# A fused attention, expert and dense kernel: joined weight blocks, a reordered attention loop, dense weights kept in SBUF, and a deferred low part

## The chip, the cores and the metric

The kernel runs on one core of a Trainium2 chip. The metric is the device time of one execution in microseconds (us). The engines are TensorE (PE in the profile, PEld its weight loads), VectorE (DVE), ScalarE (ACT), GpSimd (POOL) and SyncE (SP, which here only issues DMAs).

## The reference

Three layers follow one another, over 3072 tokens of 384 numbers.

```
state = alpha[t] * state + outer(k[t], v[t]);  y[t] = q[t] @ state      # 4 x 8 heads, 768 steps, 48 wide
e = argmax(cosine(x, expert_emb) / tau)                                 # 8 experts, one per token
x2[token] = gate[token] * (relu(x[token] @ w1[e]) @ w2[e])              # w1: 384 x 1024, w2: 1024 x 384
h = x2 @ w_in;  g = where(h > 0, h, exp(min(h, 0)) - 1);  out = g @ w_out   # 384 x 2048, 2048 x 384
```

w_in and w_out come as 64-bit floating point numbers, all else as 32-bit ones.

## The kernel before

**Attention stage.** The sequence is cut into 24 tiles of 128 steps. For a tile, two scans on VectorE make running products of alpha (R backwards, line 316, and A forwards, line 325), GpSimd scales k and q by them (Kh, line 321, and Qh, line 328), TensorE makes scores (psS, line 352), VectorE masks them from PSUM into P (line 354, two halves), and TensorE makes the output (psY), the state's update (psU) and the router's logits (psX). ScalarE copies. Every step writes its instructions by hand in one order (`manual_schedule`), and each engine takes its own in that order. In the loop of `fast()` one turn i issues: transpose of tile i+1 (`stT`), both scans of tile i+2 (`stA`) with the state's addition, router steps and the scatter of one finished tile (`put`) between them, then the scores and masks of tile i+1 (`stB`), and the outputs of tile i (`stC`). Router arithmetic comes as a list of small VectorE instructions, of which `step(n)` issues n. `put` copies the token number on GpSimd (line 522) and scatters 128 rows to a DRAM buffer sorted by expert (line 523).

**Expert stage.** `moe1` takes 64 blocks (8 experts by 8 parts of 128 hidden units). Numbers are kept as a rounded high part and a low part, so each product is three matmuls: block n issues nine of 432 columns into `h` (`mm1`), then nine of block n-1 into `y` (`mm2`). ScalarE writes the high part `hh` (line 886) and VectorE the low part `hl` (line 887), which the next `mm2` needs. Expert weights come in slots of 128 x 1536 (768 KB), two staging buffers deep, and are split in three pieces a slot: high on ScalarE (line 175), low on VectorE (line 178), into rings of eight slots; w1 and w2 have slots of their own.

In the same blocks the dense layer's 64-bit weights are turned into 32-bit ones, in 32 parts (`decode`: three integer instructions on VectorE, lines 212 to 214, a square on ScalarE, line 216, two on GpSimd) and split (`decode_end`: line 226 on ScalarE, line 227 on VectorE). Both parts are then stored to DRAM (lines 229 and 230), and in the last two experts loaded back into the ring by GpSimd's queue (`load_dense`). The buffers that a part is decoded in (`dt`, `dg`) number two; a third decode needs the first one's stores to have read them.

**Dense stage.** `moe2` takes 96 blocks (six groups of 512 tokens by 16 parts). Block n is nine matmuls of 512 columns into one of four PSUM buffers, a minimum on VectorE (`mn`, line 1032), an exponential on ScalarE, a combination on VectorE (`g`, line 1035), and high and low parts (`gh`, line 1038, `gl`, line 1039); then the twelve matmuls of block n-3 into `o`.

Of the kernel before, what the change touches and what calls it, by code (L numbers as in the profile page):

```python
# [20 lines left out]
T = 128  # L21
# [18 lines left out]
SLOT = 1536  # L40
XW = DM + 1
# [14 lines left out]
def fused_kernel(ctx, tc, qk, a, v, emb, w1, w2, wi, wo, cst, sel, cols, out):  # L56
# [5 lines left out]
    ring = ctx.enter_context(tc.tile_pool(name="ring", bufs=8))  # L62
    stage = ctx.enter_context(tc.tile_pool(name="stage", bufs=2))
# [76 lines left out]
    wq = []  # L140
    for e in range(E):
        for s in range(2):
            wq.append(("w1", e, s, w1[e, :, s * SLOT:(s + 1) * SLOT]))
        for s in range(2):
            wq.append(("w2", e, s, w2[e, :, s * SLOT:(s + 1) * SLOT]))
    raw, whi, wlo = {}, {}, {}
    nload = [0]

    def load_w(n=1):
        for _ in range(n):  # L150
            if nload[0] < len(wq):
                nm, e, s, src = wq[nload[0]]
                t = stage.tile([128, SLOT], F32, tag="raw", name="raw")
                nc.sync.dma_start(out=t, in_=src)
                raw[nload[0]] = t
                nload[0] += 1

    PIECES = 3
    pieces = [(i, j) for i in range(len(wq)) for j in range(PIECES)]
    npc = [0]  # L160

    def split_piece(lag=None):

        if npc[0] >= len(pieces):
            return
        i, j = pieces[npc[0]]
        npc[0] += 1
        nm, e, s, _ = wq[i]
        if j == 0:
            whi[nm, e, s] = ring.tile([128, SLOT], F32R, tag="whi", name="whi")  # L170
            wlo[nm, e, s] = ring.tile([128, SLOT], F32R, tag="wlo", name="wlo")
        w = SLOT // PIECES
        sl = slice(j * w, (j + 1) * w)
        h, l, r = whi[nm, e, s], wlo[nm, e, s], raw[i]
        nc.scalar.activation(out=h[:, sl], in_=r[:, sl], func=AF.Copy)  # L175
# [12 lines left out]


    HS = SLOT // 4  # L190
    dq = [(nm, j, src) for nm, src in (("wi", wi), ("wo", wo)) for j in range(4 * SLOT // HS)]
    d_hi = {nm: dram.tile([128, 4 * SLOT], F32, name=nm + "_hi") for nm in ("wi", "wo")}
    d_lo = {nm: dram.tile([128, 4 * SLOT], F32, name=nm + "_lo") for nm in ("wi", "wo")}
    dbuf = {}
# [8 lines left out]
    dpart = {}  # L203

    def decode(j, pool):
        if j >= len(dq):
            return
        w = dbuf.pop(j).bitcast(I32).rearrange("p (n two) -> p n two", two=2)
        lo, hi = w[:, :, 0], w[:, :, 1]
        t = pool.tile([128, HS], I32, name="dt")  # L210
# [8 lines left out]
        dpart[j] = (g, tf)  # L219

    def decode_end(j):
        if j not in dpart:
            return
        nm, s, _ = dq[j]
        g, tf = dpart.pop(j)
# [6 lines left out]
    def load_dense(nm, s):  # L232
        whi[nm, 0, s] = ring.tile([128, SLOT], F32R, tag="whi", name="whi")
        wlo[nm, 0, s] = ring.tile([128, SLOT], F32R, tag="wlo", name="wlo")
        nc.gpsimd.dma_start(out=whi[nm, 0, s], in_=d_hi[nm][:, s * SLOT:(s + 1) * SLOT])
        nc.gpsimd.dma_start(out=wlo[nm, 0, s], in_=d_lo[nm][:, s * SLOT:(s + 1) * SLOT])

    def wblk(nm, e, col, n):
        s, c0 = divmod(col, SLOT)
        return whi[nm, e, s][:, c0:c0 + n], wlo[nm, e, s][:, c0:c0 + n]  # L240
# [19 lines left out]
    def attention():  # L260
        with ExitStack() as st:
# [4 lines left out]
            xp = st.enter_context(tc.tile_pool(name="xp", bufs=8))  # L266
# [12 lines left out]
            ones = gp.tile([128, 1], F32, name="ones")  # L279

# [21 lines left out]
            Qh, Kh, Rs = {}, {}, {}  # L302

            def stA(i, mid):

# [4 lines left out]
                if i >= NT:  # L310
                    mid()
                    return
                al = at.pop(i)
                R = Rs[i] = wk.tile([C2, SW], F32, name="R")
                A = wk.tile([C2, SW], F32, name="A")
                nc.vector.tensor_tensor_scan(R[:, ::-1], al[:, ::-1], back[:, ::-1], 0.0, op0=ALU.mult, op1=ALU.max)
                fo = fore[i % 2]
                nc.vector.reciprocal(seg(fo)[:, :, 0:1], seg(R)[:, :, 1:2])
                x = qkt.pop(i)
                Kh[i] = wk.tile([C2, NP, T], F32, name="Kh")  # L320
                nc.gpsimd.tensor_tensor(Kh[i], x[:, 1], R[:, 1:].rearrange("c (p t) -> c p t", t=TP)[:, :, 1:], op=ALU.mult)
                step(2)
                if i < NT - 2:
                    mid()
# [5 lines left out]
                if i >= NT - 2:  # L330
                    mid()
# [838 lines left out]
```

## Time and profile before

| | us |
|---|---|
| median of 3 runs (889.39 to 891.69) | 891.16 |
| the profiled execution | 883.97 |
| its span, first to last instruction | 882.2 |
| attention stage, to 202.5 | 202.5 |
| expert stage, 202.5 to 473.4 | 270.9 |
| dense stage, 473.4 to 882.2 | 408.8 |

Busy over the span: TensorE 819.9 us (93%), VectorE 565.3 (64%), ScalarE 356.5 (40%), GpSimd 207.8 (24%). A TensorE that is busy need not be at its peak, since the end of a matmul is modelled and the granted clock changes. A `[4.27 <-ACT hh L886]` behind a row says that the engine stood idle for 4.27 us before it and that ScalarE's instruction of line 886 released it.

### The profile page before, as it was taken

What the parts mean: (1) busy time and instruction counts of PE and PEld (TensorE: products, weight loads), DVE (VectorE), ACT (ScalarE), POOL (GpSimd) and SP (SyncE); (2) the same over time, 40 slices, a digit from 0 to 9 for tenths busy, and PEclk for the clock granted to TensorE, in tenths of its full rate; (3) what the DMA queues carried; (4) which work ended last, traced back from release to release, by engine and by line L of the source; (5) the groups of instructions that cost most, each with busy time, mean ns of one, the idle gap of its engine ahead of it and who ended that gap; (6) DMA issues with size and microseconds to landing.
All of it is one profiled execution on the core that took longest, in us unless ns stands there. A gap on an engine that the chain in (4) does not pass through costs nothing.

```text
span 882.2 us, 13140 instructions
## 1 busy us (share of the span) xinstructions
PE 819.9 (93%) x4880; PEld 736.4 (83%) x4880; DVE 565.3 (64%) x1054; ACT 356.5 (40%) x739; POOL 207.8 (24%) x235
## 2 busy tenths in 40 slices
PE   7999888749997988989999999999999999999995
PEld 5888777629986987978988999999999999999995
DVE  7899999935785676867734555555555555555552
ACT  2556654614453454545523333333333333333331
POOL 6435555531233233323431001101100100100102
PEclk7898888978998999999999999999999999999999
DMA  9977795235888778978999000000000000000000
GB/s 265 311 191 192 205 261 158 55 102 184 198 241 189 183 223 208 243 208 209 307 299 214 1 1 10 27 1 9 27 1 9 29 1 4 33 0 1 37 1 36
DMA packets 47554, 107.50 MB, mean 122 GB/s; under 512 B 11880, under 2 KB 26472, under 8 KB 47472
## 3 DMA queue, kind: packets, MB, share of 16 engines
q1 hardware_dynamic: 42096, 84.46, 36.0%
q0 software_dynamic: 5376, 22.04, 7.9%
q8 instruction: 41, 0.67, 0.3%
q14 instruction: 41, 0.34, 0.1%
HBM read 81.68 MB, written 24.81 MB: 121 GB/s over the span
## 4 chain that ended last, share of the span: by engine, by line
PE 62%; DMA 8%; DVE 4%; issue 1%; ACT 1%; SPq 0%; POOLq 0%; POOL 0%; DVEq 0%; ACTq 0%
PE h L1030 22%; PE o L1052 8%; PE o L1050 8%; PE o L1051 8%; DMA wi_lo<-dt 5%; DMA wo_lo<-dt 3%; PE y L897 3%; PE y L896 3%; PE y L898 3%; PE h L881 2%; PE h L883 2%; PE h L882 2%; DVE wlo L178 1%; DVE hl L887 1%; PE t L864 1%
## 5 line engine op out<-in xcount | busy, mean ns | idle before, releaser
L1033 ACT ACTIVATE mn<-mn 128x512 f32<-128x512 f32 x96 | 60.7, 632 | 182.4 <-DVE mn L1032 182.4
L1052 PE MATMUL o<-whi,gl 128*128 128x384 f32 x384 | 129.3, 337 | 0.0
L1050 PE MATMUL o<-whi,gh 128*128 128x384 f32 x384 | 129.3, 337 | 0.0
L1051 PE MATMUL o<-wlo,gh 128*128 128x384 f32 x384 | 129.1, 336 | 0.0
L1030 PE MATMUL h<-xh,whi 128*128 128x512 f32 x288 | 112.5, 391 | 0.6 <-ACT x2T L910 0.6
L1030 PE MATMUL h<-xh,wlo 128*128 128x512 f32 x288 | 113.0, 393 | 0.0
L1039 DVE TENSOR_TENSOR gl<-g,gh 128x512 fp32r<-128x512 f32 x96 | 66.6, 694 | 72.4 <-ACT gh L1038 72.4
L1030 PE MATMUL h<-xl,whi 128*128 128x512 f32 x288 | 112.9, 393 | 0.0
L1035 DVE SCALAR_TENSOR_TENSOR g<-mn,h 128x512 f32<-128x512 f32 x96 | 66.1, 689 | 72.6 <-ACT mn L1033 72.6
L1061 POOL DMA_INDIRECT out_dram<-ob,ids x24 | 23.7, 986 | 363.3 <-DVE gl L1039 243.8
L1038 ACT ACTIVATE gh<-g 128x512 fp32r<-128x512 f32 x96 | 60.7, 632 | 77.8 <-DVE g L1035 77.0
L1032 DVE TENSOR_SCALAR mn<-h 128x512 f32<-128x512 f32 x96 | 66.2, 690 | 37.4 <-PE h L1030 37.1
L896 PE MATMUL y<-hh,whi 128*128 128x432 f32 x192 | 73.3, 382 | 9.8 <-ACT hh L886 7.8
L897 PE MATMUL y<-hl,whi 128*128 128x432 f32 x192 | 71.8, 374 | 7.9 <-DVE hl L887 7.9
L178 DVE TENSOR_TENSOR wlo<-raw,whi 128x512 fp32r<-128x512 f32 x96 | 75.6, 810 | 3.8 <-ACT whi L175 3.8
L217 POOL TENSOR_SCALAR dg<-dg 128x384 f32<-128x384 f32 x32 | 41.4, 1293 | 151.6 <-ACT dg L216 151.6
L1050 PEld LDWEIGHTS o<-whi,gh 128*128 128x128 f32 x384 | 72.1, 188 | 3.9
L1051 PEld LDWEIGHTS o<-wlo,gh 128*128 128x128 f32 x384 | 72.1, 188 | 3.8
L1052 PEld LDWEIGHTS o<-whi,gl 128*128 128x128 f32 x384 | 72.1, 188 | 0.0
L898 PE MATMUL y<-hh,wlo 128*128 128x432 f32 x192 | 70.7, 368 | 0.0
L881 PE MATMUL h<-xh,whi 128*128 128x432 f32 x192 | 70.4, 367 | 0.0
L883 PE MATMUL h<-xh,wlo 128*128 128x432 f32 x192 | 69.9, 364 | 0.0
(205 smaller groups left out, 1542.4 us busy)
## 6 DMA issues: line engine op xcount, KB each, us to landing
raw<-in_w_dram SPq DMA_DIRECT2D x32, 768.0 KB, 5.2
qk<-in_qk_dram SPq DMA_DIRECT2D x24, 448.0 KB, 8.1
vt<-in_v_dram SPq DMA_DIRECT2D x24, 352.0 KB, 6.8
raw<-in_wi_dram SPq DMA_DIRECT2D x16, 384.0 KB, 4.1
raw<-in_wo_dram SPq DMA_DIRECT2D x16, 384.0 KB, 4.6
at<-in_alpha_dram SPq DMA_DIRECT2D x24, 226.2 KB, 7.2
xr<-xs SPq DMA_DIRECT2D x7, 576.0 KB, 11.2
wi_hi<-dg SPq DMA_DIRECT2D x16, 192.0 KB, 5.8
```

Source lines behind the costliest of these rows:

```text
L178: nc.vector.tensor_tensor(l[:, sl], r[:, sl], h[:, sl].bitcast(F32), op=ALU.subtract)
L881: nc.tensor.matmul(ps, wh, xh[:, kk], start=(kk == 0), stop=False)
L883: nc.tensor.matmul(ps, wl, xh[:, kk], start=False, stop=(kk == KD - 1))
L896: nc.tensor.matmul(acc[e][d], wh, hh, start=(f == 0), stop=False)
L897: nc.tensor.matmul(acc[e][d], wh, hl, start=False, stop=False)
L898: nc.tensor.matmul(acc[e][d], wl, hh, start=False, stop=(f == FB - 1))
L1030: nc.tensor.matmul(ps, l, x, start=(n == 0), stop=(n == len(terms) - 1))
L1032: nc.vector.tensor_scalar(mn, ps, 0.0, None, op0=ALU.min)
L1039: nc.vector.tensor_tensor(gl, g, gh.bitcast(F32), op=ALU.subtract)
L1050: nc.tensor.matmul(o_, gh[:, sl], wh, start=(f == 0), stop=False)
L1051: nc.tensor.matmul(o_, gh[:, sl], wl, start=False, stop=False)
L1052: nc.tensor.matmul(o_, gl[:, sl], wh, start=False, stop=(f == M - 1))
```

## The change

- **Weights.** w1 and w2 are joined in one array, a hidden block's w1 columns beside its w2 rows, so that a slot of 1536 columns holds two whole blocks. Loads are of a piece (512 columns, 256 KB), six staging buffers in all, and each split piece issues the load of the sixth after it. The rings have four slots. In the expert stage splits begin at block 3.
- **Dense weights.** The decoded 32-bit parts stay in SBUF (`dense`, 18 buffers of 128 x 768). `decode_end`, its stores and `load_dense` are gone. `split_dense` makes high and low parts: a few in the last expert blocks, the others in the first group of the dense stage, two in most blocks. 64-bit loads are issued a block later than their buffer's decode.
- **Attention loop.** `stA` becomes `stR` (scan R, Kh) and `stA` (scan A, Qh), `stB` becomes `stS` (scores) and `stP` (one mask). A turn issues scores first; VectorE's order becomes R, state, first mask, A, second mask, then router steps and the weights' low part. The scatter stands between the first mask and A. The token number is copied by ScalarE, and GpSimd writes a 1 x 1 zero (`tick`) in its place.
- **Dense stage.** A block's low part `gl` is issued behind the next block's minimum and exponential (`flush`). The first token group's input lies in tiles of 128 x 512 rather than 128 x 3 x 512.
- The expert input `xr` has a buffer of its own from the start, used for all experts.

```diff
-    ring = ctx.enter_context(tc.tile_pool(name="ring", bufs=8))
-    stage = ctx.enter_context(tc.tile_pool(name="stage", bufs=2))
+    ring = ctx.enter_context(tc.tile_pool(name="ring", bufs=4))
+    stage = ctx.enter_context(tc.tile_pool(name="stage", bufs=2 * PIECES))
...
         def low_part():
-            nc.vector.tensor_tensor(l[:, sl], r[:, sl], h[:, sl].bitcast(F32), op=ALU.subtract)
-            if j == PIECES - 1:
-                raw.pop(i)
-                if i != AHEAD - 1:
-                    load_w()
+            nc.vector.tensor_tensor(l[:, sl], r, h[:, sl].bitcast(F32), op=ALU.subtract)
+            load_w()
...
-    def decode_end(j):
...
-        nc.scalar.activation(out=g.bitcast(F32R), in_=tf, func=AF.Copy)
-        nc.vector.tensor_tensor(tf, tf, g, op=ALU.subtract)
-        sl = slice(s * HS, (s + 1) * HS)
-        nc.sync.dma_start(out=d_hi[nm][:, sl], in_=g)
-        nc.sync.dma_start(out=d_lo[nm][:, sl], in_=tf)
...
+    def split_dense(nm, m, dense):
...
+        nc.scalar.activation(out=h, in_=r, func=AF.Copy)
+        nc.vector.tensor_tensor(l, r, h.bitcast(F32), op=ALU.subtract)
...
             def put(i, apart=True):
...
-                nc.gpsimd.tensor_copy(x[:, DM:], c["tok"][:, i:i + 1])
+                if apart and puts:
+                    nc.gpsimd.memset(tick, 0.0)
...
+                    stS(i + 1)
                     stT(i + 1)
...
-                    stA(i + 2, mid)
-                    if putq and i >= tail - 2:
+                    stR(i + 2)
+                    stG(i - 1)
+                    stP(i + 1, 0)
+                    if putq and place[putq[0]][0] in gated:
                         put(putq.pop(0))
-                    stB(i + 1)
+                    stA(i + 2)
+                    stP(i + 1, 1)
...
-                split_piece()
-                if n % 2:
+                if n > 2:
                     split_piece()
+                    if n % 2:
+                        split_piece()
+                if freed:
+                    load_d(freed.pop(), dc)
                 j = (n - 2) * 4 // 7
                 if j >= 0 and j != (n - 3) * 4 // 7:
-                    decode_end(j - 1)
-                    decode(j, dc)
-                    load_d(j + 2, dc)
+                    decode(j, dc, dense)
+                    freed.append(j + 2)
...
                 nc.scalar.activation(out=mn, in_=mn, func=AF.Exp)
+                flush()
                 g = e_p.tile([128, U], F32, name="g")
...
-                nc.vector.tensor_tensor(gl, g, gh.bitcast(F32), op=ALU.subtract)
+                low.append(lambda: nc.vector.tensor_tensor(gl, g, gh.bitcast(F32), op=ALU.subtract))
...
+                    if u == 0:
+                        split_dense("wi", m + 4, dense)
+                        split_dense("wo", m + 2, dense)
```

What this makes of the order on an engine, at three places. First VectorE in one turn of the attention loop, one with router steps, before:

```order
L316 SCALAR_TENSOR_TENSOR R<-at,back 112x517
L318 RECIPROCAL fore_127<-R 112x4
L502 TENSOR_TENSOR t<-psR,oh 128x32
L503 TENSOR_REDUCE pos<-t 128x4
L391 TENSOR_TENSOR G_123<-psU,G_123 112x4x112
L421 TENSOR_REDUCE lg<-psX 128x8
L325 SCALAR_TENSOR_TENSOR A<-at,fore_127 112x517
L504 TENSOR_SCALAR pos_i<-pos 128x4
L100 TENSOR_SCALAR rs_y<-ss 128x4
L354 TENSOR_TENSOR P<-psS,cs 128x512
L101 TENSOR_SCALAR rs_y<-rs_y 128x4
```

and in such a turn of the changed kernel (psU, psX, psR and psS lie in PSUM):

```order
L311 SCALAR_TENSOR_TENSOR R<-at,back 112x517
L312 RECIPROCAL fore_126<-R 112x4
L394 TENSOR_TENSOR G_122<-psU,G_122 112x4x112
L358 TENSOR_TENSOR P<-psS,cs 128x512
L321 SCALAR_TENSOR_TENSOR A<-at,fore_126 112x517
L358 TENSOR_TENSOR P<-psS,cs 128x512
L424 TENSOR_REDUCE lg<-psX 128x8
L505 TENSOR_TENSOR t<-psR,oh 128x32
L506 TENSOR_REDUCE pos<-t 128x4
L507 TENSOR_SCALAR pos_i<-pos 128x4
```

One mask now stands between the scans, and all router steps stand behind the second mask. On GpSimd, a turn is Kh, copy, scatter, Qh before and Kh, tick, scatter, Qh now.

Second, SyncE's queue in the second expert's blocks, before (wi_hi and wi_lo are the DRAM copies of the dense weights):

```order
L229 DMA wi_hi<-dg 128x384
L230 DMA wi_lo<-dt 128x384
L200 DMA raw_5439<-in_wi_dram 128x384
L154 DMA raw<-in_w_dram 128x1536
L229 DMA wi_hi<-dg 128x384
L230 DMA wi_lo<-dt 128x384
```

and now:

```order
L156 DMA raw<-in_w_dram 128x512 x3
L196 DMA raw_5488<-in_wi_dram 128x384
L156 DMA raw<-in_w_dram 128x512 x3
L196 DMA raw_5581<-in_wi_dram 128x384
L156 DMA raw<-in_w_dram 128x512
```

Only loads are left in it. Third, VectorE in the first blocks of the dense stage, before:

```order
L1032 TENSOR_SCALAR mn<-h_8143 128x512
L1035 SCALAR_TENSOR_TENSOR g<-mn,h_8143 128x512
L1039 TENSOR_TENSOR gl<-g,gh 128x512
L1032 TENSOR_SCALAR mn<-h_8174 128x512
L1035 SCALAR_TENSOR_TENSOR g<-mn,h_8174 128x512
```

and now (wd holds decoded weights, dwi and dwo their high parts, dlo their low parts):

```order
L231 TENSOR_TENSOR dlo<-wd,dwo 128x384
L1046 TENSOR_SCALAR mn<-h_8250 128x512
L1054 TENSOR_TENSOR gl<-g,gh 128x512
L1050 SCALAR_TENSOR_TENSOR g<-mn,h_8250 128x512
L231 TENSOR_TENSOR dlo<-wd,dwi 128x384
L231 TENSOR_TENSOR dlo<-wd,dwo 128x384
L1046 TENSOR_SCALAR mn<-h_8285 128x512
```

`gl` of the block before stands between `mn` and `g`, and two low parts of weights behind `g`.

## Rows read from the trace of the kernel before

**Rows 1.** Stages: stretch, length, busy us (instructions) by engine, granted clock, DMA.
```profile
0.00:202.50 202.50, 167.73 (x1629) 142.07 (x1629) 172.20 (x430) 95.65 (x267) 97.04 (x107) 0.86 0.68 193
202.50:473.40 270.90, 252.59 (x1237) 231.12 (x1236) 179.92 (x307) 125.84 (x252) 81.88 (x79) 0.97 0.84 222
473.40:882.20 408.80, 399.61 (x2016) 363.20 (x2016) 213.20 (x318) 134.96 (x221) 28.92 (x50) 1.00 0.06 20
```

**Rows 2.** Waits of TensorE in the expert stage: total us, times, longest.
```profile
PE y L897 <- DVE hl L887: 7.9, 8, 1.7
PE y L896 <- ACT hh L886: 7.8, 4, 4.3
```

**Rows 3.** Groups of VectorE, expert stage: busy, mean ns, idle before, releasers.
```profile
L227 DVE TENSOR_TENSOR dt<-dt,dg 128x384 f32<-128x384 f32 x32 | 18.2, 570 | 1.3 <-ACT dg L226 1.2
...
L212 DVE TENSOR_SCALAR dt<-raw 128x384 int32<-128x384 int32 x32 | 16.0, 501 | 37.3 <-DMA wi_lo<-dt 18.8 <-DMA wo_lo<-dt 18.5
```

**Rows 4.** The same of ScalarE.
```profile
L216 ACT ACTIVATE dg<-raw 128x384 f32<-128x384 f32 x32 | 17.6, 549 | 41.0 <-DMA wi_hi<-dg 21.1 <-DMA wo_hi<-dg 12.5 <-issue 5.0
L226 ACT ACTIVATE dg<-dt 128x384 fp32r<-128x384 f32 x32 | 16.6, 517 | 6.5 <-POOL dt L218 6.4
```

**Rows 5.** Timeline around one stall of TensorE: start, length, instruction, idle before.
```profile
273.31 0.32 SPq L230 DMA_DIRECT2D wi_lo<-dt  x1
...
276.99 0.54 ACT L216 ACTIVATE dg<-raw 128x384 f32<-128x384 f32 x1 [7.08 <-DMA wi_hi<-dg]
...
278.00 0.73 PE L896 MATMUL y<-hh,whi 128*128 128x432 f32 x1 [4.27 <-ACT hh L886]
```

**Rows 6.** Stretches of the expert stage: its start, behind that stall, an undisturbed one.
```profile
200.00:205.00 5.00, 5.00 (x17) 4.42 (x18) 1.21 (x2) 1.06 (x2) 0.00 (x0) 0.50 0.69 224
...
280.00:285.00 5.00, 5.00 (x16) 4.61 (x17) 4.44 (x8) 0.98 (x2) 1.83 (x3) 0.57 0.78 193
355.00:380.00 25.00, 25.00 (x130) 23.19 (x129) 20.56 (x36) 14.67 (x30) 8.05 (x7) 1.00 0.89 214
```

**Rows 7.** Timeline of VectorE in one turn of the attention loop.
```profile
138.42 1.23 DVE L316 TENSOR_TENSOR_SCAN R<-at,back 112x517 f32<-112x517 f32 x1
...
140.71 1.35 DVE L325 TENSOR_TENSOR_SCAN A<-at,fore 112x517 f32<-112x517 f32 x1
...
142.11 0.68 DVE L354 TENSOR_TENSOR P<-psS,cs 128x512 f32<-128x512 f32 x1
142.71 1.88 DVE L101 TENSOR_SCALAR rs_y<-rs_y 128x4 int32<-128x4 int32 x1
144.62 0.17 DVE L105 SCALAR_TENSOR_TENSOR rs_t<-rs_y,ss 128x4 f32<-128x4 f32 x1
...
145.99 1.24 DVE L316 TENSOR_TENSOR_SCAN R<-at,back 112x517 f32<-112x517 f32 x1
```

**Rows 8.** Timeline of GpSimd in the same turn.
```profile
140.92 1.12 POOL L522 COPY xt<-cs 128x1 f32<-128x1 f32 x1
142.32 1.02 POOL L523 DMA_INDIRECT xs<-xt,pos_i  x1 [0.28 <-DVE rs_y L100]
143.36 1.19 POOL L328 TENSOR_TENSOR Qh<-qk,A 112x512 f32<-112x512 f32 x1
```

**Rows 9.** The attention loop as one stretch, columns as in the first group.
```profile
15.00:165.00 150.00, 133.61 (x1422) 118.62 (x1423) 144.55 (x290) 80.63 (x230) 73.36 (x71) 0.88 0.75 210
```

**Rows 10.** Two scatters in a row at the end of attention, GpSimd.
```profile
179.62 0.99 POOL L523 DMA_INDIRECT xs<-xt,pos_i  x1 [0.28 <-POOL xt L522]
...
181.08 0.99 POOL L523 DMA_INDIRECT xs<-xt,pos_i  x1 [0.28 <-POOL xt L522]
```

**Rows 11.** Timeline of the dense stage's first block, and TensorE's first use of gl.
```profile
475.92 0.69 DVE L1032 TENSOR_SCALAR mn<-h 128x512 f32<-128x512 f32 x1 [0.71 <-PE h L1030]
...
477.31 0.69 DVE L1035 SCALAR_TENSOR_TENSOR g<-mn,h 128x512 f32<-128x512 f32 x1 [0.70 <-ACT mn L1033]
...
478.03 0.63 ACT L1038 ACTIVATE gh<-g 128x512 fp32r<-128x512 f32 x1 [0.75 <-DVE g L1035]
...
482.21 0.34 PE L1052 MATMUL o<-whi,gl 128*128 128x384 f32 x1
```

More of the change, by code (lines that the diff above doesn't have):

```diff
@@ L137, in inv_norm1 @@
         return y, steps
[L140 to L145, printed above, removed]
+    wq = [(e, s) for e in range(E) for s in range(FB * FW // SLOT)]
+    pieces = [(e, s, j) for e, s in wq for j in range(PIECES)]
     raw, whi, wlo = {}, {}, {}
     nload = [0]
+    npc = [0]
     def load_w(n=1):
         for _ in range(n):
[L151 to L154, printed above, removed]
+            if nload[0] < len(pieces):
+                e, s, j = pieces[nload[0]]
+                t = stage.tile([128, PW], F32, tag="raw", name="raw")
+                nc.sync.dma_start(out=t, in_=w12[e, :, s * SLOT + j * PW:s * SLOT + (j + 1) * PW])
                 raw[nload[0]] = t
                 nload[0] += 1
-    PIECES = 3
-    pieces = [(i, j) for i in range(len(wq)) for j in range(PIECES)]
-    npc = [0]
     def split_piece(lag=None):
@@ L187, in split_piece, with wblk @@
             lag.append(low_part)
-    HS = SLOT // 4
+    def wblk(e, col, n):
+        s, c0 = divmod(col, SLOT)
+        return whi[e, s][:, c0:c0 + n], wlo[e, s][:, c0:c0 + n]
+    HS = DM
     dq = [(nm, j, src) for nm, src in (("wi", wi), ("wo", wo)) for j in range(4 * SLOT // HS)]
-    d_hi = {nm: dram.tile([128, 4 * SLOT], F32, name=nm + "_hi") for nm in ("wi", "wo")}
-    d_lo = {nm: dram.tile([128, 4 * SLOT], F32, name=nm + "_lo") for nm in ("wi", "wo")}
-    dbuf = {}
+    dbuf, dec, dhi, dlo = {}, {}, {}, {}
     def load_d(j, pool):
@@ L201, in load_d, with decode @@
             dbuf[j] = t
-    dpart = {}
-    def decode(j, pool):
+    def decode(j, pool, dense):
         if j >= len(dq):
             return
+        nm, s, _ = dq[j]
+        d, r = divmod(s * HS, DS)
+        if r == 0:
+            dec[nm, d] = dense.tile([128, DS], I32, tag="wd", name="wd")
+        t = dec[nm, d][:, r:r + HS]
         w = dbuf.pop(j).bitcast(I32).rearrange("p (n two) -> p n two", two=2)
         lo, hi = w[:, :, 0], w[:, :, 1]
-        t = pool.tile([128, HS], I32, name="dt")
         g = pool.tile([128, HS], F32, name="dg")
@@ L279, in attention @@
             ones = gp.tile([128, 1], F32, name="ones")
+            tick = gp.tile([1, 1], F32, name="tick")
             qkt, at = {}, {}
@@ L352, in stB, with stP @@
                         nc.tensor.matmul(s[h2][:, p], kh[rows, p], qh[rows, p], start=True, stop=True)
-                for h2 in range(2):
-                    nc.vector.tensor_tensor(P[i][:, h2], s[h2], c["tri"][:, None, :].to_broadcast([128, NP, T]), op=ALU.mult)
-                    step(2)
+            def stP(i, h2):
+                if i >= NT:
+                    return
+                if h2 == 0:
+                    P[i] = wk.tile([128, 2, NP, T], F32, name="P")
+                nc.vector.tensor_tensor(P[i][:, h2], sc[i][h2], c["tri"][:, None, :].to_broadcast([128, NP, T]), op=ALU.mult)
             yT = {}
@@ L625, in fast @@
                 nc.gpsimd.memset(zero, 0.0)
-                stA(0, lambda: None)
-                stH(0)
-                stA(1, lambda: None)
-                stH(1)
+                for j in range(2):
+                    stR(j)
+                    stA(j)
+                    stE(j)
+                    stH(j)
                 rows, rtau = emb_t[:, :2 * NP * HP], emb_t[:, 2 * NP * HP:]
@@ L754, in ending @@
                     put(j)
-                xr = stage.tile([128, 4, DM], F32, tag="raw", name="xr0")
+                xr = xr_p.tile([128, 4, DM], F32, name="xr")
                 load_rows(xr, 0, [0, 128, 256, DM], puts[:-1])
@@ L904, in mm2 @@
                         for nm in ("xh2", "xl2"):
-                            first.append(stage.tile([128, KD, U], F32R, tag="raw", name=nm))
+                            first.append([stage.tile([128, U], F32R, tag="raw", name=nm) for _ in range(KD)])
                     nc.scalar.activation(out=x2T[:, 0, bass.ds(o1, CAP)], in_=y[0], func=AF.Copy)
@@ L1009, in moe2, with flush @@
             x2, gb, acc, stores = {0: first}, {}, {}, []
+            low = []
+            def flush():
+                while low:
+                    low.pop()()
             def load_u(u):
@@ L1014, in load_u @@
                 if u % 2:
-                    xh, xl = (x_p.tile([128, KD, U], F32R, tag=nm, name=nm) for nm in ("xh2", "xl2"))
+                    xh, xl = ([x_p.tile([128, U], F32R, tag=nm, name=nm) for _ in range(KD)] for nm in ("xh2", "xl2"))
                 else:
-                    xh, xl = (stage.tile([128, KD, U], F32R, tag="raw", name=nm) for nm in ("xh2", "xl2"))
+                    xh, xl = ([stage.tile([128, U], F32R, tag="raw", name=nm) for _ in range(KD)] for nm in ("xh2", "xl2"))
                 for kk in range(KD):
@@ L1094, in fused_kernel @@
         with tc.manual_schedule():
-            first = moe1(x2T, *x0)
+            dense = es.enter_context(tc.tile_pool(name="dense", bufs=18))
+            first = moe1(x2T, *x0, dense)
             shared.close()
-            moe2(x2T, first)
+            moe2(x2T, first, dense)
 _OUTS = [((N, DM), "float32")]
```

190 lines of the change are left out of this document (97 added, 93 removed).

## The prediction

> **What bounds the kernel now.** I read the stages first [rows 1]. The dense stage takes 408.8 us, and TensorE is busy for 399.6 of them at full clock (the rest is the end of the last group): 4.16 us for each of 96 blocks. Nothing outside TensorE can shorten it. The expert stage takes 270.9 us, TensorE is idle for 18.3 of them and its clock is 0.97. In the attention stage VectorE is the fullest engine.
>
> Next the waits of the expert stage. TensorE waits for `hl` and `hh`, the two parts of a block's hidden units [rows 2]. That is not the cause: VectorE and ScalarE were late because both stood in the decoding of the dense weights, waiting for a DMA. Line 212 has 37.3 us of idle time in front of it, nearly all ended by the stores of wi_lo and wo_lo [rows 3]; line 216 has 41.0, of which 33.6 end with the stores of wi_hi and wo_hi [rows 4]. One case shows the chain [rows 5]: SyncE issues the store of wi_lo at 273.31, ScalarE stands for 7.08 us until a buffer is free, its `hh` comes late, and TensorE starts at 278.00 after 4.27 us. Behind that stall its clock is 0.57 and 16 matmuls go through in 5 us, where an undisturbed stretch has 130 in 25 us, or 5.2 a microsecond [rows 6]. So a stall is paid twice, in idle time and in the slower time behind it.
>
> Last the attention loop: 150 us of which VectorE is busy for 144.55 and TensorE for 133.61 [rows 9]. VectorE's share is not all work. In one turn, a small router instruction takes 1.88 us where its neighbour of the same size takes 0.17 [rows 7]. It ends at 144.59, and GpSimd's Qh, which reads two SBUF operands, ends at 144.55 [rows 8]: it was held until Qh let go. The masks P, which read one operand from PSUM, are not held beside GpSimd.
>
> **Expert stage.** It holds 1237 matmuls [rows 1]. At the undisturbed rate these take 1237 / 5.2 = 237.9 us, so 33.0 us of the stage are idle or slow. The change takes away what causes this: no store reads the decode buffers, so a third decode waits only for VectorE, ScalarE and GpSimd themselves. 64 stores and 16 loads leave the queues, and the weights' loads no longer stand behind them. Work goes too: line 227 (18.2 us of VectorE) and line 226 (16.6 us of ScalarE) move to other places [rows 3, 4]. What is left is (179.9 - 18.2) / 238 = 68% of VectorE's time and (125.8 - 16.6) / 238 = 46% of ScalarE's, and in the undisturbed stretch, with more than that on both, TensorE stood in nothing. What stays: the slow start, where 17 matmuls take 5 us [rows 6], about half of it in the stage, 1.5 us; and blocks in which two pieces, a decode and a turned input fall together, which I put at 2.5. Gain 33.0 - 1.5 - 2.5 = 29 us. At most it is 31.5; at least 15, if half of the waits come back in another form.
>
> The cover that shrinks is the ring, eight slots to four. A slot is refilled from the block in which its last matmuls have been issued, and is needed 3.5 blocks later, 3.5 x 3.7 = 13 us. The refill is three pieces. Low and high part of 384 columns take 0.57 and 0.52 us [rows 3, 4], so a piece of 512 some 1.45 and three 4.4 us. That fits three times over, and the six loads in flight cover as much again.
>
> **Attention loop.** The turn in the rows took 145.99 - 138.42 = 7.57 us [rows 7]. Its loss begins on GpSimd: the copy of the token number stood from 140.92 to 142.04 [rows 8], until scan A ended at 142.06; then came the scatter, 1.02 us, and only then Qh, which held VectorE until 144.55. With the copy gone the scatter can run beside A, if the `tick` is not held as the copy was. No row shows a GpSimd write beside a scan, so the price lies between that of the copy, 1.12 us, and its unhindered 0.1 to 0.2; I take the low end, since the tick reads nothing and the held instructions in these rows all read SBUF. Qh then starts at A's end. One mask, 0.6 us, and reductions out of PSUM hide half of it, and what follows is held for 0.5 to 0.7 us where it was 1.7: a gain of 1.0 in the 13 turns that the code gives a scatter, 13 us. Against it: a second mask has moved in front of A, so in the nine other turns, where two masks hid Qh, half a microsecond of it is bare, 4.5 us; and TensorE, 89% busy, will not always have the scores ready for the first mask, 1.5 us. Sum: 7 us gained. The bounds are 16, where TensorE's own busy time is reached, and a loss of 4, if the tick is held.
>
> The Trainium skill (SBUF — State Buffer, "Who interferes with whom") says that a VectorE instruction with two SBUF inputs contends with a GpSimd one that reads SBUF and not with one that only writes it. By it the tick passes and the sum stays 7; by the opposite the loop loses 4. The held copy agrees with its first half; its second half no row shows.
>
> **End of attention.** Eight scatters in a row are 181.08 - 179.62 = 1.46 us apart, 0.99 of it the scatter, 0.47 copy and gap [rows 10]. A tick on another tile needs no gap in front of the scatter. At most 8 x 0.47 = 3.8 us go, at least none if ScalarE, which now writes the token numbers, becomes late. I take 2, and the rest of this end, the first expert's rows from DRAM and the branches, unchanged.
>
> **Dense stage.** Deferring `gl` cannot itself gain time, since TensorE does not wait there. It makes room for the weights' splits in the first group. Worked out from one block [rows 11]: from `mn` to `g` 1.39 us, in which `gl` of the block before (0.69, as `g`) fits; from `g` to `gh` 0.72, `gh` 0.63, then two high parts of 0.517 [rows 4], so the second is done 475.92 + 1.39 + 0.72 + 0.63 + 1.03 = 479.69; the last low part takes 0.57 [rows 3], and the next `mn` can start at 480.26. That is 4.34 us a block against TensorE's 4.16: 0.18 x 12 blocks = 2.2 us behind. The next group's six input splits fall into block 8, some 3 x 0.69 = 2.1 us on VectorE. The cover is what TensorE leaves before it needs the first `gl`: 482.21 - (480.26 + 0.69) = 1.3 us. So 2.2 + 2.1 - 1.3 = 3 us lost. From nothing, if ScalarE's parts overlap better, to 10, if the two low parts stand one behind the other (0.57 more in each block). In the other 80 blocks VectorE has 2.1 us of work and nothing waits.
>
> **Sum.** -29 - 7 - 2 + 3 = -35 us. On the profiled execution's 883.97 that is 849; the three timed runs lie 7.2 us above it, by 0.8%, so I take the difference off their median: 856 us.
>
> **Rivals.**
> *The tick is held by scan A as the copy was.* For it: the copy was. Against: it reads nothing. The loop then loses 4: -29 + 4 - 2 + 3 = -24, 867 us.
> *The expert stage's waits return.* VectorE's heaviest blocks are as long as TensorE's, and a late `hl` stops `mm2` at once. Against: the undisturbed stretch carried more. Half the gain: -15 - 7 - 2 + 3 = -21, 870 us.
> *All covers hold:* expert stage -31.5, loop -16, end -3.8, dense 0: -51, 840 us.
> *The dense stage's first group is slower:* +10 in place of 3: 863 us.
> *Slower than before: the ring of four.* If ScalarE's first piece of a slot waits for `mm2` with other work behind it on that in-order queue, `hh` is late, TensorE stalls and its clock falls as behind 278 us. There are 32 slots. The other terms give 6, so the stage would have to reach 270.9 + 6, which is 37.5 us over 239.4, or 1.2 us a slot; at 2 us a slot it is 239.4 + 64 - 270.9 - 6 = +26, 918 us. Against it stands the cover of 13 us over 4.4.
>
> **How the numbers follow.** Forecast 50%, tick held 15%, waits return 14%, all covers hold 13%, dense stage slower 4%, ring slower 4%. The likeliest is 856. Its own range, with a few microseconds either way in the loop and the dense stage, is 849 to 864. For 8 in 10 I add the two cases around 868 and leave out most of the case at 840 and the slow one: 842 to 872. A difference within 0.3%, 2.7 us, can't be told from none. Only the ring case is slower, 4%; 2% for a mixture that ends within 0.3%; faster 94%.
>
> **What would show it.** In the changed profile: no DMA among what ends VectorE's and ScalarE's waits at the decode; the expert stage near 242 us with clock 1.0 after its first 5 us; the scatter starting before A ends, and router instructions of under 0.9 us beside Qh; the loop near 143 us; in the dense stage's first group, `gl` behind the next `mn` and TensorE waiting for `gl` or `g` by a few tenths in some blocks from about the seventh on. The prediction is wrong if TensorE still stalls for more than a microsecond at a time among the experts, if ticks last as long as A, or if the loop's turns with scatter stay at 7.5 us.

## The result and the profile after

The changed kernel takes 861.18 us (median of 4 runs, 858.38 to 864.15) where the kernel before takes 891.42 on the same chip: a ratio of 0.9646, with a 95% interval of 0.9581 to 0.9711. The forecast was 856, in a range of 842 to 872. The profiled execution took 860.85 us, with a span of 858.9. Its difference to the profile of before is 23.3 us of span; the medians differ by 30, since the profiled execution of before lay 7.2 us under its median and this one on it. The steps of the prediction are held against the two profiles, where 35 us were forecast; in which stage the other 7 us of the medians lie, no profile shows.

The stages of the changed kernel, as in [rows 1] (the borders are again the first matmul of the experts and of the dense layer):

```profile
0.00:199.96 199.96, 160.35 (x1628) 138.95 (x1628) 161.96 (x430) 100.68 (x291) 97.17 (x106) 0.85 0.70 200
199.96:450.26 250.30, 243.48 (x1237) 225.50 (x1236) 167.73 (x279) 114.07 (x224) 73.62 (x65) 1.00 0.61 149
450.26:858.90 408.64, 399.30 (x2016) 361.54 (x2016) 219.14 (x346) 146.59 (x249) 29.33 (x47) 1.00 0.03 12
```

Nearly all of it comes from the expert stage: 270.9 us became 250.3. The attention stage gave 2.5, the dense stage 0.2. In the expert stage TensorE's idle time fell from 18.3 to 6.8 us and its mean clock rose from 0.97 to 1.00. A little of that is chance: only in this profile did the stage begin at full clock (26 matmuls in 5 us); in that of before and in all those below it began with 16 to 21 at 0.53 to 0.75. What TensorE still waits for there, against [rows 2]:

```profile
PE y L907 <- ACT hh L897: 3.3, 2, 1.7
PE y L908 <- DVE hl L898: 2.9, 4, 0.8
```

So fewer and shorter waits, and the same two operands. The reason behind them is a new one. VectorE's and then ScalarE's waits for a DMA at the decode, where [rows 3] and [rows 4] had the stores of the decoded weights:

```profile
DVE wd L210 <- DMA raw<-in_wi_dram: 10.5, 4, 4.0
DVE wd L210 <- DMA raw<-in_wo_dram: 6.9, 4, 4.1
```

```profile
ACT dg L214 <- DMA raw<-in_wi_dram: 15.9, 5, 4.8
ACT dg L214 <- DMA raw<-in_wo_dram: 10.5, 5, 4.9
```

No store is among them any more, but the 64-bit weights themselves arrive late. One case, in the way of [rows 5]: SyncE, then VectorE, ScalarE and TensorE in the same stretch.

```profile
254.93 1.11 SPq L246 DMA_DIRECT2D xr<-xs  x2
256.74 0.33 SPq L156 DMA_DIRECT2D raw<-in_w_dram  x1
257.12 0.42 SPq L196 DMA_DIRECT2D raw<-in_wi_dram  x1
```

```profile
269.75 0.36 DVE L210 TENSOR_SCALAR wd<-raw 128x384 int32<-128x384 int32 x1 [4.01 <-DMA raw<-in_wi_dram]
```

```profile
269.81 0.55 ACT L214 ACTIVATE dg<-raw 128x384 f32<-128x384 f32 x1 [4.79 <-DMA raw<-in_wi_dram]
270.26 0.51 ACT L897 ACTIVATE hh<-h 128x432 fp32r<-128x432 f32 x1
```

```profile
270.83 0.46 PE L907 MATMUL y<-hh,whi 128*128 128x432 f32 x1 [1.58 <-ACT hh L897]
```

The load is issued at 257.12, a block behind the decode that freed its buffer (VectorE's last read of it ended at 254.82) and close behind the next expert's rows (`xr`). It takes 12.6 us, where the median of the sixteen loads of w_in is 4.4, and the decode gets it at 269.75. The `hh` of the running block stands behind the decode's `dg` on ScalarE, in program order, and TensorE waits for it. It is the chain of [rows 5] with a load in the place of a store.

The attention loop. GpSimd in the turn that answers to [rows 8], and VectorE in the same turn, which answers to [rows 7]:

```profile
139.51 0.09 POOL L527 MEMSET tick<- 1x1 f32 x1
139.76 1.78 POOL L528 DMA_INDIRECT xs<-xt,pos_i  x1 [0.16 <-issue]
141.56 1.20 POOL L323 TENSOR_TENSOR Qh<-qk,A 112x512 f32<-112x512 f32 x1
```

```profile
139.50 1.22 DVE L321 TENSOR_TENSOR_SCAN A<-at,fore 112x517 f32<-112x517 f32 x1
140.64 0.67 DVE L358 TENSOR_TENSOR P<-psS,cs 128x512 f32<-128x512 f32 x1
141.75 1.04 DVE L507 TENSOR_SCALAR pos_i<-pos 128x4 int32<-128x4 f32 x1
```

The tick passes beside A in 0.09 us, as forecast, and the scatter starts before A ends. But then the scatter takes 1.78 us in place of 1.02: scan A ends at 140.72, and Qh starts 0.84 us behind it instead of with it. The router instruction beside Qh takes 1.04 us; it was 1.88 [rows 7] and was to be under 0.9. This turn takes 7.35 us (scan R at 137.03 and at 144.38) in place of 7.57.

At the loop's start VectorE stands for the alphas, which it hardly did before:

```profile
33.36 1.24 DVE L311 TENSOR_TENSOR_SCAN R<-at,back 112x517 f32<-112x517 f32 x1 [3.73 <-DMA at<-in_alpha_dram]
```

Where the loop gained and lost is told by the starts of scan R, one in each of its 22 turns. The tenth and the last, before and then now:

```profile
70.27 1.22 DVE L316 TENSOR_TENSOR_SCAN R<-at,back 112x517 f32<-112x517 f32 x1
...
158.99 1.23 DVE L316 TENSOR_TENSOR_SCAN R<-at,back 112x517 f32<-112x517 f32 x1
```

```profile
72.94 1.23 DVE L311 TENSOR_TENSOR_SCAN R<-at,back 112x517 f32<-112x517 f32 x1
...
155.99 1.22 DVE L311 TENSOR_TENSOR_SCAN R<-at,back 112x517 f32<-112x517 f32 x1
```

The first is at 13.27 and 13.24. So the first nine turns, nearly all without a scatter, lost 2.7 us, and the next twelve, nearly all with one, gained 5.7, or 0.47 a turn. In the three other profiles with this loop, below, the nine lost 0.0 to 1.3 us and the twelve gained 5.4 to 6.0.

The dense layer's first group, where [rows 11] stood: VectorE in one block, and TensorE's one wait for `gl` in the whole stage.

```profile
482.29 0.69 DVE L1046 TENSOR_SCALAR mn<-h 128x512 f32<-128x512 f32 x1
482.89 0.69 DVE L1054 TENSOR_TENSOR gl<-g,gh 128x512 fp32r<-128x512 f32 x1
483.74 0.69 DVE L1050 SCALAR_TENSOR_TENSOR g<-mn,h 128x512 f32<-128x512 f32 x1 [0.16 <-ACT mn L1047]
485.60 0.56 DVE L231 TENSOR_TENSOR dlo<-wd,dwi 128x384 fp32r<-128x384 f32 x1 [1.17 <-ACT dwi L230]
...
486.54 0.68 DVE L1046 TENSOR_SCALAR mn<-h 128x512 f32<-128x512 f32 x1
```

```profile
PE o L1067 <- DVE gl L1054: 1.4, 1, 1.4
```

`gl` stands where VectorE used to wait for ScalarE's exponential [rows 11]; two low parts stand behind `g` (the second is left out above), and a block takes 486.54 - 482.29 = 4.25 us (4.34 were forecast).

### The profile page after: what moved, and what is told of

Its sections match the earlier page's. It is cut to its first block, busy times and chain, and to the rows that moved or that the text cites. A ratio compares the mean times of both kernels' runs of the same rounds, so it can differ in the third digit from the quotient of the medians.

```text
span 858.9 us, 13084 instructions
## 1 busy us (share of the span) xinstructions
PE 803.1 (94%) x4880; PEld 726.0 (85%) x4880; DVE 548.8 (64%) x1054; ACT 361.3 (42%) x763; POOL 200.1 (23%) x218
## 4 chain that ended last, share of the span: by engine, by line
PE 63%; DMA 5%; DVE 4%; ACT 3%; issue 1%; SPq 0%; POOLq 0%; POOL 0%; DVEq 0%; ACTq 0%
PE h L1044 20%; PE o L1067 7%; PE o L1065 7%; PE o L1066 7%; PE y L907 4%; PE y L908 3%; DMA raw<-in_wi_dram 3%; PE h L892 3%; PE h L894 3%; PE y L909 3%; PE h L893 3%; DMA raw<-in_wo_dram 1%; PE t L875 1%; DVE dlo L231 1%; DVE g L1050 1%
## 5 line engine op out<-in xcount | busy, mean ns | idle before, releaser
L1067 PE MATMUL o<-dwo,gl 128*128 128x384 f32 x384 | 129.5, 337 | 1.5 <-DVE gl L1054 1.4
L1066 PE MATMUL o<-dlo,gh 128*128 128x384 f32 x384 | 128.3, 334 | 0.0
L1065 PE MATMUL o<-dwo,gh 128*128 128x384 f32 x384 | 128.3, 334 | 0.0
L1044 PE MATMUL h<-xh,dwi 128*128 128x512 f32 x288 | 112.9, 392 | 0.6 <-ACT x2T L921 0.6
L1044 PE MATMUL h<-xh,dlo 128*128 128x512 f32 x288 | 113.1, 393 | 0.0
L1044 PE MATMUL h<-xl,dwi 128*128 128x512 f32 x288 | 112.5, 392 | 0.0
L1065 PEld LDWEIGHTS o<-dwo,gh 128*128 128x128 f32 x384 | 72.0, 187 | 4.2
L1066 PEld LDWEIGHTS o<-dlo,gh 128*128 128x128 f32 x384 | 72.0, 187 | 4.0
L898 DVE SCALAR_TENSOR_TENSOR hl<-h,hh 128x432 fp32r<-128x432 f32 x64 | 38.7, 605 | 55.8 <-ACT hh L897 55.8
L1067 PEld LDWEIGHTS o<-dwo,gl 128*128 128x128 f32 x384 | 72.2, 188 | 2.4 <-DVE gl L1054 2.1
```

The lines of the kernel that those rows point to most:

```text
L1044: nc.tensor.matmul(ps, l, x, start=(n == 0), stop=(n == len(terms) - 1))
L1065: nc.tensor.matmul(o_, gh[:, sl], wh, start=(f == 0), stop=False)
L1066: nc.tensor.matmul(o_, gh[:, sl], wl, start=False, stop=False)
L1067: nc.tensor.matmul(o_, gl[:, sl], wh, start=False, stop=(f == M - 1))
```

## The experiments

The theory: the decode's wait for its stores, gone with the change, has come back as a wait for its loads, which is all that keeps the expert stage from the forecast 242 us; and the attention loop gained less than forecast since scan A holds the scatter, and since its first loads are late. The rivals: blocks that are too full for VectorE and ScalarE whatever the DMAs do, and a loop bound by something else. The changed kernel again, the third buffer, the scatter behind Qh and the weights one piece a turn ran on one chip (before: 888.68 us); the four decode buffers, the token number, the undone deferral and the four edits together ran on another (before: 889.8), on which the changed kernel itself was not run. Each ratio is to the kernel before on the same chip.

**The changed kernel again, for comparison.**

> The changed kernel as it is, beside its variants on the same chip. Near 861 us: first matmul of the experts at 200.0, of the dense stage at 450.3, expert stage 250.3 us long, dense stage 408.6.

860.81 us, ratio 0.9684 [0.9659, 0.9708]; attention stage 198.93, expert stage 254.09, dense stage 408.68 in its profile. The expert stage varies by some 4 us from profile to profile, with 249.4 to 254.1 over the six profiles in which its code is that of the changed kernel; the waits for the 64-bit weights are in both profiles of the changed kernel itself. Of the 254.1 a part is slower time behind stalls: the clock is 0.93 to 0.97 in three of the four stretches of 25 us between 250 and 350, where it is 1.00 in all four of the profile above.

**A third buffer for the 64-bit weights.**

```
-  t = pool.tile([128, HS], I64, bufs=2, name="raw64")
+  t = pool.tile([128, HS], I64, bufs=3, name="raw64")
...
   load_d(1, dc)
+  load_d(2, dc)
...
-  freed.append(j + 2)
+  freed.append(j + 3)
```

> A third buffer for the 64-bit dense weights, loaded three ahead. Theory (the store wait has become a load wait): the waits for in_wi and in_wo at the decode, 17.4 us on VectorE and 26.4 on ScalarE, nearly go, TensorE's idle time in the expert stage falls from 6.8 to under 2 us, the stage from 250.3 to 240 to 244, the kernel is 6 to 10 us shorter than the changed one. Rival (blocks in which two pieces, a decode and a turned input meet are simply too full for VectorE and ScalarE): TensorE's waits for hh and hl stay at 5 us or more and the stage at 248 to 251, though the loads are on time.

854.08 us, ratio 0.9606 [0.9581, 0.963], an interval clear of the changed kernel's on the same chip (0.9659 to 0.9708). In its expert stage no wait of TensorE for an operand is left, and no DMA is among VectorE's or ScalarE's:

```profile
197.49:441.38 243.89, 243.27 (x1237) 227.13 (x1237) 167.22 (x279) 114.36 (x224) 73.43 (x65) 0.99 0.63 151
```

The same work on VectorE (167 us) and ScalarE (114 us) as in the changed kernel, and 0.6 us of idle time on TensorE. Full blocks are refuted; the late loads are shown. What makes them late is not taken apart by this run, which gives a buffer more and asks for each load a decode earlier. In the changed kernel's profile the four loads that lie on the critical chain (issued at 233.29, 257.12, 294.82 and 321.96) all follow an `xr` in SyncE's queue, and three of them take 9.9 to 12.7 us.

**The kernel before with four decode buffers**, and nothing else of the change:

```
-  dc = st.enter_context(tc.tile_pool(name="dc", bufs=2))
+  dc = st.enter_context(tc.tile_pool(name="dc", bufs=4))
```

> The kernel before with four buffers in place of two for the decoded high and low parts that the stores read; stores, loads, ring and loop as they were. Theory (the waits of the decode for its stores are what TensorE's stalls in the expert stage come from): the waits of VectorE and ScalarE for wi_lo, wo_lo, wi_hi and wo_hi, 37.3 and 33.6 us, fall to under 8 in all, TensorE's idle time of 18.3 us to under 8, expert stage 270.9 to 248 to 258, the kernel 12 to 22 us shorter than before. Rival (64 stores and 16 loads fill the queues, so the loads of pieces and 64-bit weights are late in their place): the stage stays over 262.

862.05 us, ratio 0.97 [0.9653, 0.9747]: one number in the kernel before does as much as the whole change, whose own ratio can't be told from this one. Its expert stage, and its decode lines that answer to [rows 3] (VectorE) and [rows 4] (ScalarE):

```profile
207.03:451.34 244.31, 243.54 (x1238) 227.05 (x1237) 180.96 (x307) 126.81 (x252) 84.29 (x79) 0.99 0.91 247
```

```profile
L212 DVE TENSOR_SCALAR dt<-raw 128x384 int32<-128x384 int32 x32 | 19.0, 595 | 1.2 <-DMA raw<-in_wi_dram 1.2
```

```profile
L216 ACT ACTIVATE dg<-raw 128x384 f32<-128x384 f32 x32 | 17.5, 546 | 3.2 <-DMA raw<-in_wi_dram 3.0 <-DMA raw<-in_wo_dram 0.2
```

The stage is shorter than the theory's 248 to 258. The 64 stores, the 16 loads back, 181 us of VectorE and a DMA share of 0.91 are all still there, and TensorE is idle for 0.8 us. What the stage before paid for was the wait for a buffer that a store still read; the store's bytes and the split work on VectorE cost nothing as long as the engines are not made to stand. Its waits for the 64-bit weights are small too (1.2 and 3.2 us), with two buffers for them as in the changed kernel, but with each load asked for in the block of its decode.

The attention stage was 4.5 us longer in this profile than in that of before (207.03 against 202.49). 3.3 of them lie behind the loop's last scan R, where ScalarE stands 3.05 us in front of its last copy `yT`. All four profiles from this chip have such a stand, of 2.7 to 4.1 us; in the six others it is 0.3 at most. So attention stages of these four and of the others can't be compared without it. What holds ScalarE there is open.

**GpSimd's scatter behind Qh.**

```
-  if putq and place[putq[0]][0] in gated:
-      put(putq.pop(0))
   stA(i + 2)
+  if putq and place[putq[0]][0] in gated:
+      put(putq.pop(0))
   stP(i + 1, 1)
```

> In the attention loop GpSimd issues tick and scatter behind Qh in place of ahead of it. Theory (a scatter that begins beside scan A takes 1.78 us and so starts Qh 0.8 us late, which VectorE pays at its first router instruction): Qh starts at A's end, turns with a scatter are 0.5 to 0.8 us shorter in 13 turns, the attention stage ends 5 to 9 us earlier. Rival (another instruction takes the scatter's place, Kh of the next turn starts later, or TensorE is the bound): the stage ends within 2 us of 200.0. If a scatter is held by router instructions with two SBUF inputs too, it takes 1.5 us or more there as well; if scan A alone does it, near 1.0.

853.71 us, ratio 0.9609 [0.958, 0.9637], again clear of the changed kernel's; the attention stage ends at 193.06. GpSimd in two of its turns, and VectorE's instructions beside Qh and beside the second scatter:

```profile
136.44 1.18 POOL L323 TENSOR_TENSOR Qh<-qk,A 112x512 f32<-112x512 f32 x1 [1.35 <-DVE A L321]
...
137.81 1.01 POOL L528 DMA_INDIRECT xs<-xt,pos_i  x1
...
144.87 1.83 POOL L528 DMA_INDIRECT xs<-xt,pos_i  x1 [0.16 <-issue]
```

```profile
135.07 1.23 DVE L321 TENSOR_TENSOR_SCAN A<-at,fore 112x517 f32<-112x517 f32 x1
...
137.32 0.32 DVE L507 TENSOR_SCALAR pos_i<-pos 128x4 int32<-128x4 f32 x1
...
144.65 1.22 DVE L311 TENSOR_TENSOR_SCAN R<-at,back 112x517 f32<-112x517 f32 x1
```

Qh starts at 136.44, 0.14 us behind A's end (135.07 + 1.23), and the router instruction that took 1.04 takes 0.32. The scatter at 137.81 runs beside small router instructions and takes 1.01; the one at 144.87 begins beside scan R and takes 1.83. So either scan holds a scatter, and the small instructions do not. But length is not what counts: the low part of the expert weights, 0.68 us with two SBUF inputs, holds four scatters of this profile as well, which take 1.35 to 1.53. One of them, VectorE and then GpSimd:

```profile
104.17 0.68 DVE L175 TENSOR_TENSOR wlo<-raw,whi 128x512 fp32r<-128x512 f32 x1
```

```profile
104.21 1.52 POOL L528 DMA_INDIRECT xs<-xt,pos_i  x1
```

The twelve turns of the loop that took 88.72 us before and 83.05 in the changed kernel take 78.37 here.

**The token number by GpSimd again**, in place of the tick.

```
   def scale_x(i):
...
-      nc.scalar.activation(out=x[:, DM:], in_=c["tok"][:, i:i + 1], func=AF.Copy)
   def put(i, apart=True):
...
-      if apart and puts:
-          nc.gpsimd.memset(tick, 0.0)
+      nc.gpsimd.tensor_copy(x[:, DM:], c["tok"][:, i:i + 1])
```

> The changed kernel with the token number written by GpSimd ahead of the scatter again, in place of the tick (ScalarE no longer writes it). Theory (the tick is free, but the scatter behind it is held by scan A as the copy was): the copy ends with A and the scatter, 1.0 us, behind it, so Qh starts 1.05 us behind A's end in place of 0.84: 0.2 x 13 = 2.7 us in the loop and 0.2 x 8 = 1.6 at the end of attention, stage 199 to 200 becomes 202 to 205. Rival of the prediction (moving the copy is worth 1.0 us a turn): 209 or later. Rival (nothing): within 1.5 us of 199.5.

866.66 us, ratio 0.9737 [0.9703, 0.9772]; the attention stage ends at 206.07, between the theory's 202 to 205 and the prediction's 209. This is the chip with ScalarE's stand; against the other profile from it that has the changed loop (the undone deferral, 201.85) the stage is 4.2 us longer, as the theory's 4.3. GpSimd in one turn (scan A ran from 134.78 to 136.01):

```profile
134.80 1.18 POOL L525 COPY xt<-cs 128x1 f32<-128x1 f32 x1
136.26 1.02 POOL L526 DMA_INDIRECT xs<-xt,pos_i  x1 [0.28 <-DVE A L321]
137.31 1.19 POOL L323 TENSOR_TENSOR Qh<-qk,A 112x512 f32<-112x512 f32 x1
```

The copy is held until A ends, as in [rows 8]; 0.28 us pass before the scatter, which the expectation had left out, and Qh starts 1.30 us behind A: 0.46 later than in the changed kernel, or 0.46 x 13 = 6.0 us. The loop agrees: the twelve turns that took 83.05 in the changed kernel take 88.23 us, against 82.74 with the tick on the same chip, so 5.5 us, and 88.72 before. So the moved copy is worth 5.5 to 6.0 us, against the 13 forecast for it, and nearly all that these turns gained.

**The first expert weights, one piece a turn.**

```
-  if i == 1:
-      load_w(2 * PIECES)
+  if 2 <= i < 2 + 2 * PIECES:
+      load_w()
```

> The six expert-weight loads that the changed kernel issues in one turn of the attention loop (5.29 us of SyncE from 19.41, alphas and vectors queued behind them) are issued one a turn from the second turn on. Theory (late start-up loads): the waits of scan R for the alphas, 3.73 us at 33.36 and 1.67 at 39.90, and the 1.91 for psU at 43.25 go; the attention stage ends 4 to 7 us earlier, at 193 to 196, and the kernel is 4 to 7 us shorter than the changed one. Rival (the bytes in flight are the same, other loads and the zero fill are what is late, or the loop's later turns take it back): the stage ends within 1.5 us of 200.0.

859.35 us, ratio 0.9674 [0.9646, 0.9702], not told apart from the changed kernel; the attention stage ends at 197.63. The waits for alphas go, and others take their place on VectorE and TensorE:

```profile
40.54 0.62 DVE L396 COPY G<-psU 112x448 f32<-112x448 f32 x1 [2.81 <-PE psU L382]
```

```profile
35.98 1.11 PE L419 MATMUL psX<-rhsX,yT 128*128 128x104 f32 x8 [2.15 <-DVE lg L424]
```

VectorE now waits 2.81 us for `psU`; TensorE was late with it since it had itself stood for the logit reductions `lg`, which the change moved behind A and both masks. So the late loads at the loop's start cost about a microsecond, not four. The stage ends 2.4 us before 200.0, outside the rival's 1.5 too, but the third buffer's run, which has the loads as they were, ends it at 197.49 on the same chip: by that the rival holds.

**The deferral of gl undone.**

```
-  low.append(lambda: nc.vector.tensor_tensor(gl, g, gh.bitcast(F32), op=ALU.subtract))
+  nc.vector.tensor_tensor(gl, g, gh.bitcast(F32), op=ALU.subtract)
```

> The changed kernel with the deferral of gl undone: in the dense layer VectorE subtracts gl right behind its gh, as before the change. Theory (the deferral pays for the weights' splits of the first group): VectorE then stands for gh in each block, a block of the first group is mn 0.69, exp 0.70, g 0.69, gh 0.63, gl 0.69 and two low parts of 0.57 in a row = 4.5 us against TensorE's 4.16, so the first group loses about 0.38 x 12 = 4.6 us and 2.1 more at the input splits, less a cover of 1.3: dense stage 411 to 415, attention and expert stages as in the changed kernel. Rival (ScalarE's high parts and the six blocks of slack carry it anyway): dense stage 408.0 to 409.5.

872.22 us, ratio 0.9801 [0.9766, 0.9836]; the dense stage takes 416.70 us, 8 more than in the changed kernel and 2 more than the theory's upper end. VectorE in one block of its first group, then TensorE's longest wait in the stage:

```profile
480.17 0.69 DVE L1054 TENSOR_TENSOR gl<-g,gh 128x512 fp32r<-128x512 f32 x1 [0.76 <-ACT gh L1053]
...
483.16 0.69 DVE L1050 SCALAR_TENSOR_TENSOR g<-mn,h 128x512 f32<-128x512 f32 x1 [0.76 <-ACT mn L1047]
484.61 0.69 DVE L1054 TENSOR_TENSOR gl<-g,gh 128x512 fp32r<-128x512 f32 x1 [0.76 <-ACT gh L1053]
```

```profile
PE o L1065 <- ACT ob L1073: 5.0, 1, 5.0
```

A block takes 484.61 - 480.17 = 4.44 us: VectorE waits 0.76 twice, for the exponential and for `gh`, and in the changed kernel `gl` fills the first of these. That is 0.19 us a block more than there. The late blocks end in one stall of 5.0 us at 535.63, for the copy of a finished group, and TensorE's clock is 0.95 from 530 to 600, where it is 1.00 in the changed kernel. So the loss is paid mostly at one place. This rests on one profile.

**Four edits together:** the third buffer, the scatter behind Qh, the weights one piece a turn, and in the loop's fourth turn the logit reductions ahead of scan A.

```
+  if i == 3:
+      while late:
+          late.pop(0)()
   stA(i + 2)
```

> The changed kernel with four edits: scatter behind Qh, a third buffer for the 64-bit weights, the first expert weights one piece a turn, and in the fourth turn the two logit reductions in front of scan A (TensorE waited 2.15 us for them there). If the gains add up: attention stage 190 to 193, expert stage 244, dense stage 408.6, together 843 to 846 of span. If one takes the other's place (the expert stage's first loads late, or the loop bound by VectorE alone): 848 to 853.

849.62 us, ratio 0.9548 [0.9514, 0.9581], the fastest of all. Its expert stage takes 244.54 us, its dense stage 408.32, its attention stage:

```profile
0.00:193.74 193.74, 154.97 (x1628) 132.60 (x1628) 156.64 (x430) 100.11 (x291) 89.00 (x106) 0.87 0.75 208
```

The span, 846.6 us, falls in between the two expectations. The two edits at the loop's start bring a late scan R forward, to 116.55 from 118.37 with the scatter's edit alone, and the last one to 146.45 from 150.49, but the attention stage is no shorter than there (193.06): their gain is lost behind the loop. It is lost to the stand of ScalarE that all profiles from this chip have. Here it is in front of the last `yT`, then the same copy in the third buffer's profile, from the other chip:

```profile
164.81 0.60 ACT L376 ACTIVATE yT<-psY 128x512 f32<-128x512 f32 x1 [4.12 <-remote]
```

```profile
169.37 0.60 ACT L376 ACTIVATE yT<-psY 128x512 f32<-128x512 f32 x1 [0.32 <-PE psY L374]
```

So this run does not show that the gains take each other's place.

## Why the prediction was right, point by point

**Expert stage, forecast -29, measured -20.6 in the first profile.** The reading was right: stores held the decode, the decode held `hh` and `hl`, and the undisturbed rate was the measure of what could be had. The kernel before with four decode buffers shows the first (stage 244.3), the changed kernel with a third load buffer the second (243.9, so -27.0 against the forecast's -29). The last 2 are two errors against each other. The rate of 5.2 was read too high, since a stretch also counts the matmuls that lie across its borders: eleven stretches that cover this run's stage count 1255, the stage as a whole 1237. Those took 243.3 busy us, 5.1 a microsecond, so the stage is some 4 us longer than reckoned. Of the 2.5 us put aside for full blocks, only 0.6 came, as idle time. What failed is the sentence "a third decode waits only for VectorE, ScalarE and GpSimd themselves". It left out the load of the 64-bit weights: a decode needs a full buffer as well as a free one, and the change issues its load a block later, behind pieces and `xr` in one queue. That took back 6.4 us here, 6.6 to 10.2 in the three other profiles from the third buffer's chip; how much of it is the block and how much the queue was not tested apart. It is also one of the signs that the prediction named for being wrong: TensorE still stalls for more than a microsecond at a time among the experts, 1.7 at the longest. The rival "waits return" named the size but not the cause: its full blocks do not exist, as the third buffer shows. The ring of four slots cost nothing: without the late loads TensorE waits for no weight.

**Attention loop, forecast -7; end of attention, forecast -2; measured -2.5 together** (attention stages of 197.5 to 201.9 us in the four profiles with this loop, against 202.5). The tick was free, as forecast. The failed step is "Qh then starts at A's end": the scatter ahead of it is stretched to 1.78 us by scan A, so a turn with a scatter gained 0.47 us where 1.0 was forecast, 5.7 in twelve turns. The kernel before had a row that could have told: its one scatter that begins beside a scan (the scan ran from 158.99 to 160.22, see the row above) takes 1.71 us:

```profile
159.33 1.71 POOL L523 DMA_INDIRECT xs<-xt,pos_i  x1 [1.55 <-DVE P L354]
```

The scatter behind Qh gets Qh to A's end, in most turns, and brings the stage to 193.06. Against the gain the forecast put 6 us, 4.5 for bare halves in nine turns and 1.5 for late scores. They were not tested apart, but the nine turns lost 0 to 2.7 us in all, part of it the wait for the alphas, which the prediction did not have. So both terms of the loop were too large, with opposite signs, and that their sum came within 1 to 4 us (3.0 to 5.9 gained from the first scan R to the last, in the four profiles) is partly luck. At the end the eight scatters are 1.26 us apart in place of the 1.46 of [rows 10]: the copy's 0.19 became the tick's 0.09, and of the gap of 0.28, which was to go, 0.21 stayed. With one longer gap among them the first and the eighth are 9.51 us apart in place of 10.22, and the first matmul shows nothing of it that can be told from the loop's.

**Dense stage, forecast +3, measured -0.2.** The direction of the deferral was right and its worth was the largest surprise: without it the stage is 8 us longer. The term itself was too high since the block takes 4.25 us and not 4.34 (+1.1 over 12 blocks), the splits of the inputs cost one wait of 1.4 us, and of both the stage as a whole shows nothing. The waits of a few tenths from the seventh block on did not come; there was one, at the group's input splits. The prediction gave no number for what the deferral itself is worth.

**Sum.** On the profiles -23.3 in place of -35, with both large terms short for reasons that are now shown. On the medians the miss is 5 us, because the correction by 0.8%, taken from one profiled execution of before, did not hold for the changed kernel: that execution was a quick one. The range held the time with room, and for a part of that the offset is to be thanked, not the sum: without it the forecast would have been 849, 12 us short of the profiled execution.

**The rule on the tick.** The Trainium skill (SBUF — State Buffer, "Who interferes with whom") says that VectorE with two SBUF inputs contends with a GpSimd instruction that reads SBUF, not with one that only writes. The tick's 0.09 us beside scan A agrees with the second half, which no row of before showed. The scatter is the case that the prediction did not ask about: it reads its row numbers from SBUF, so the first half covers it, and the 1.78 us beside A, 1.83 beside R, 1.52 beside the weights' low part and 1.01 beside none of them agree with that; whether it is held at these reads or at something that it writes, no run here tells apart. Had the rule been applied to the scatter as well as to the tick, Qh's late start would have been forecast.

## What to carry to other kernels

When a change removes a wait, list every event that the waiting instruction needs (a free buffer, a full buffer, an operand), and time the next latest of them by its issue, not by its engine. Before restructuring for a buffer wait, try one or two more buffers: here two more gave as much as the whole change. And an instruction moved beside a long one must be checked against the same rule as the one that it replaces, here the scatter as well as the tick.

## What the runs showed of the hardware that was not expected

An indirect scatter on GpSimd takes 0.96 to 1.03 us alone, beside the masks or beside small VectorE instructions (the first of a loop 1.14 to 1.16). When it begins beside a VectorE instruction with two SBUF inputs that is well under way, it ends 0.8 to 1.0 us behind that one: 1.71 to 1.93 us beside a scan of 112x517, 1.35 beside a low part of 128x512 that runs for 0.68. When the two begin within 0.04 us of each other, it takes 1.01 us in some cases and 1.52 to 2.01 in others. Its mean over 22 scatters was 1.04 us before, one of them beside a scan, and 1.42 in the changed kernel. Stores and loads that kept the DMA engines busy for a share of 0.91 of the expert stage did not slow TensorE, once no engine had to stand for them: 244.3 us, against 243.9 with a share of 0.63.
